# Attention and a two-layer feed-forward block on one core: the seven-product second layer used from the third group of tokens on

## The chip, the core and the metric

One NeuronCore of a Trainium2 chip runs the whole program. TensorE (PE) multiplies matrices, VectorE (DVE) and ScalarE (ACT) work element by element, GpSimd (POOL) does additions in on-chip memory, and SyncE (SP) issues most of the transfers. The metric is device time in microseconds (us); lower is better. About 0.3% (2.5 us) is what a measurement of this kernel can tell from no change.

## The reference, cut to what matters

Attention runs in blocks of 64 tokens in 64 (batch, head) pairs; its output, 4608 tokens of 512 numbers, goes through two weight matrices with a function of one number between them. All in 32-bit floating point.

```python
scores = scale * np.matmul(q_c, k_c.transpose(0, 1, 2, 4, 3))   # blocks of 64 x 64
scores = scores - np.max(scores, axis=-1, keepdims=True)
attn = np.exp(scores)
attn = attn / (np.sum(attn, axis=-1, keepdims=True) + 1e-09)
out = np.matmul(attn, v_c)
...
x = np.ascontiguousarray(attn_out.transpose(0, 2, 1, 3)).reshape(B * S, H * D)   # 4608 x 512
...
h = x @ w_in            # 512 -> 2048: the first layer
g = h - np.tanh(h)
return (g @ w_out).astype(np.float32)   # 2048 -> 512: the second layer
```

## The kernel before, in words

The 4608 tokens are 36 tiles of 128 ("pairs"), in 9 groups of four (`SIZES`). Each group goes through attention, the first layer and the second layer. The 2048 inner columns are 16 blocks of 128 (`FC = 16`); one block of one group is called a unit here. Every 32-bit operand is split into a high part (`h`, `wh`, `gh`, `xh`) and a low rest (`l`, `wl`, `gl`, `xl`), and a product is three matmuls: high by high, high by low, low by high.

There are three ways of doing the two layers.

- Groups 0 and 1: `FeedForward` with both layers in the 32-bit format of TensorE (`F32R`). One unit is `gemm1` (12 matmuls of 512 columns, L572), then `shrink` (tanh on ACT, subtraction on DVE into `t`, L583 and L584), `split` (`gh` on ACT L591, `gl` on DVE L592), and two units later `gemm2` (12 matmuls of 512 columns, L601).
- Group 2: `FeedForward` with `half` set. The first layer takes weights and tokens as pairs of 16-bit numbers, the second layer stays in 32 bits.
- Groups 3 to 8: `Fast`. Both layers take 16-bit pairs, and the second layer is a two-by-two block product done with seven products instead of eight (`Fast.gemm2`, L709: 21 matmuls of 256 columns for two tiles and two blocks of inner columns). GpSimd makes the seven sums of the left operand in every unit (L678 to L680).

What the later ways need is prepared while earlier groups run. `Half.convert` rewrites one block of first-layer weights in 16 bits: two ACT and two DVE instructions (L490, L491, L493, L494); its rest goes over the low part of the same block. `Half.combine` makes the sums of the second-layer weights for a pair of blocks j and j + 8 on GpSimd (L506 to L517), and `Half.shorten` rounds the four sums to 16-bit pairs (ACT L534, DVE L535). Before these, `Half.powers` finds a power of two by which the weights are scaled, from sums of squares (`square`, L110) through a reduction over the partitions on GpSimd. `Late` is the attention of groups 2 to 8: a scale per group (`sums`, `halves`, `across`, `spread_out`), then for each half group b `split` of q, k and v (L353, L354), `scores` on PE (L364), `shifted` (DVE L381, L382), `exponent` (ACT), `totals` (DVE L396), `divided` (DVE L404), `transpose` (ACT, DVE L411 and a transposing transfer) and `values` (PE L364, DVE L432).

In the kernel before, all 16 converts, the attention of group 2 and 16 of the 32 squares lie beside group 1. All combines but the last two and their shortens, and the attention of group 3, lie beside group 2. From group 3 on, only the attention of the next group lies beside the running group.

The order of the instructions has three sources. The first part of the program (up to the bar in `PLAN`) and everything from group 2 on is in written order (`tc.manual_schedule`): every engine takes its instructions in the order in which the code issues them. In between (the rest of group 0 and group 1) a scheduler sets the order by data and rank. In the written part `ahead` and the loops around it put steps into a table `at`: key 2s comes behind `gemm1` and `shrink` of unit s, key 2s + 1 behind the `gemm2` of that unit. `FeedForward.written` is the loop of a unit: split of the unit before, `gemm1`, `shrink`, the steps of 2s, `gemm2` of the unit two back, the steps of 2s + 1. So DVE has, in every unit, first `t`, then what the table put there, then `gl`, then the next `t`.

## Time and profile before

| what | us |
|---|---|
| three runs | 820.85, 820.67, 818.77 (median 820.67) |
| the profiled execution | 818.66, with a span of 816.9 from the first to the last instruction |
| group 0 ends: its first output store | 126.7 from the span's start |
| group 1 ends: its first output store | 219.6 |
| group 2 ends: its last output store | 321.1 |
| last output store issued | 814.0 |
| TensorE busy | 803.5 |
| VectorE busy | 644.5 |
| ScalarE busy | 467.4 |
| GpSimd busy | 381.1 |

The span is what the engines' instructions cover; the remaining 1.8 us of the profiled execution lie around it. TensorE's granted clock is 0.998 of full speed over the span. In the profile's rows "L601 PE MATMUL po<-wh,gh" is line 601, the engine, the operation and output from inputs by tile name. A chain row gives the start, the length and what the end of the program goes back to at that time; a timeline row gives start, length, the instruction, and in brackets the engine's idle time before it and what ended it. A row of the stage table gives the busy time of every engine in a stretch of the span, with the number of instructions in brackets. Two instructions that follow one another at once on one engine overlap by some 0.1 us in the records, so that a sum of lengths is a little above the time taken. One unit (one block of inner columns) is the beat to look for: 16 in each group.

### The profile page before, as it was taken

The page shows a single profiled execution, that of the slowest core. Times are in us where ns is not written, and L with a number is a line of the kernel's source. Part 1 is how long each engine was busy: PE and PEld are TensorE (multiplying, and loading weights), DVE is VectorE, ACT ScalarE, POOL GpSimd, SP SyncE. Part 2 cuts the span into 40 slices and gives each one's busy share as a digit, 9 for nine tenths or more (in the row PEclk, how much of TensorE's full clock was granted, in tenths as well). Part 3 has the DMA queues.
Part 4 walks back from the last instruction along what each step waited for, and adds up shares of the span by engine and source line. Part 5 has one row for each costly group of instructions (what it writes and reads, how often), then busy time and mean ns, then how long its engine had stood idle before and what let it go on. Part 6 is the DMA issues. An engine that isn't in the chain of part 4 may idle for free.

```text
span 816.9 us, 20560 instructions
## 1 busy us (share of the span) xinstructions
PE 803.5 (98%) x8805; PEld 664.6 (81%) x8805; DVE 644.5 (79%) x853; ACT 467.4 (57%) x754; POOL 381.1 (47%) x385
## 2 busy tenths in 40 slices
PE   8999999999999999999999999999999999999997
PEld 5677787788756568888888888888888888888886
DVE  6899986877459999797879787878887887877553
ACT  5698779665345457564745474546554655454332
POOL 2000000000028666856665756575666665757563
PEclk9999999999999999999999999999999999999999
DMA  7954523321201113122222322222222220202000
GB/s 250 344 180 156 187 86 140 105 53 34 71 1 30 49 37 120 27 79 53 80 53 79 53 79 53 79 53 79 52 80 52 79 53 2 53 3 52 2 27 26
DMA packets 58459, 63.19 MB, mean 77 GB/s; under 512 B 32768, under 2 KB 38912, under 8 KB 58368
## 3 DMA queue, kind: packets, MB, share of 16 engines
q1 hardware_dynamic: 57792, 61.10, 25.1%
q8 instruction: 69, 1.13, 0.6%
q10 hardware_dynamic: 576, 0.79, 0.3%
q14 instruction: 22, 0.18, 0.1%
HBM read 45.09 MB, written 9.44 MB: 67 GB/s over the span
## 4 chain that ended last, share of the span: by engine, by line
PE 80%; DVE 10%; ACT 5%; POOL 2%; issue 2%; DVEq 0%; ACTq 0%
PE ph L669 29%; PE po L709 26%; PE po L601 10%; PE ph L572 10%; PE psa L364 3%; PE ph L854 1%; DVE w L151 1%; DVE gl L592 1%; DVE w L152 1%; ACT wh L155 1%; ACT s L228 1%; ACT w L146 1%; ACT junk L110 1%; DVE wh L535 1%; PE psa L193 1%
## 5 line engine op out<-in xcount | busy, mean ns | idle before, releaser
L669 PE MATMUL ph<-xh,wl 128*128 128x256 f16 x2160 | 249.5, 273 | 0.0
L669 PEld LDWEIGHTS <-wl 128*128 128x128 f16 x2160 | 209.8, 98 | 25.2 <-issue 0.5
L678 POOL TENSOR_TENSOR xl<-xl 128x256 f32<-128x256 f32 x96 | 97.1, 1011 | 183.8 <-DVE xl L677 182.9
L676 ACT ACTIVATE t<-ph,sig 128x512 f32<-128x512 f32 x96 | 65.8, 685 | 147.6 <-PE ph L669 146.9
L677 DVE SCALAR_TENSOR_TENSOR xl<-ph,sig,t 128x512 f32<-128x512 f32 x96 | 71.6, 746 | 46.5 <-ACT t L676 46.3
L709 PEld LDWEIGHTS <-wh 128*128 128x128 f16 x1008 | 98.7, 98 | 11.4
L679 POOL TENSOR_TENSOR xl<-xl 128x128 f32<-128x128 f32 x96 | 105.5, 1099 | 0.0
L680 POOL TENSOR_TENSOR xl<-xl 128x256 f32<-128x256 f32 x96 | 93.1, 970 | 0.0
L709 PE MATMUL po<-wl,wh 128*128 128x256 f16 x576 | 89.7, 273 | 0.0
L690 DVE SCALAR_TENSOR_TENSOR wh<-xl,to_g,wh 128x896 f16<-128x896 f32 x48 | 64.6, 1346 | 30.0 <-ACT wh L689 30.0
L689 ACT ACTIVATE wh<-xl,to_g 128x896 f16<-128x896 f32 x48 | 49.9, 1039 | 60.8 <-POOL xl L680 60.8
L601 PE MATMUL po<-wh,gh 128*128 128x512 f32 x192 | 79.5, 414 | 1.0 <-ACT gh L591 0.8
L690 DVE SCALAR_TENSOR_TENSOR gl<-xl,to_g,gh 128x896 f16<-128x896 f32 x48 | 71.8, 1496 | 9.1 <-ACT gh L689 8.9
L601 PE MATMUL po<-wl,gh 128*128 128x512 f32 x192 | 75.7, 394 | 0.9 <-POOL wl L159 0.9
L572 PE MATMUL ph<-xh,wl 128*128 128x512 f16 (+2 forms) x316 | 76.5, 380 | 0.0
L601 PE MATMUL po<-wh,gl 128*128 128x512 f32 x192 | 75.1, 396 | 1.0 <-DVE gl L592 1.0
L709 PE MATMUL po<-wh,wh 128*128 128x256 f16 x432 | 75.9, 273 | 0.0
L709 PEld LDWEIGHTS <-gh 128*128 128x128 f16 x672 | 64.9, 98 | 7.8
L709 PE MATMUL po<-wh,gh 128*128 128x256 f16 x336 | 54.4, 273 | 0.0
L709 PE MATMUL po<-wl,gh 128*128 128x256 f16 x336 | 52.4, 273 | 0.0
L592 DVE TENSOR_TENSOR gl<-t,gh 128x512 fp32r<-128x512 f32 (+1 forms) x50 | 40.0, 800 | 15.5 <-ACT gh L591 15.3
L689 ACT ACTIVATE gh<-xl,to_g 128x896 f16<-128x896 f32 x48 | 49.5, 1032 | 4.2 <-POOL xl L680 4.1
(159 smaller groups left out, 1402.5 us busy)
## 6 DMA issues: line engine op xcount, KB each, us to landing
raw<-w_in SPq DMA_DIRECT2D x16, 512.0 KB, 3.7
raw<-w_out SPq DMA_DIRECT2D x16, 512.0 KB, 4.6
rawk<-kL SPq DMA_DIRECT2D x28, 256.0 KB, 3.9
rawv<-vL SPq DMA_DIRECT2D x28, 256.0 KB, 3.6
xl<-qL SPq DMA_DIRECT2D x28, 256.0 KB, 2.9
out<-wh SPq DMA_DIRECT2D x46, 128.0 KB, 1.8
q<-qE SPq DMA_DIRECT2D x8, 256.0 KB, 5.2
v<-vE SPq DMA_DIRECT2D x8, 256.0 KB, 4.5
```

The source lines that it names most:

```text
L572: nc.tensor.matmul(ph, lhsT=self.weight(fc, 0, a)[:, kc * P:(kc + 1) * P], rhs=x[b][:, kc, cols], start=(k == 0), stop=(k == 3 * KC - 1))
L592: nc.vector.tensor_sub(gl, t, gh)
L601: nc.tensor.matmul(self.po[t], lhsT=gg[a][:, ts], rhs=self.weight(fc, 1, b), start=(fc == 0 and i == 0), stop=(fc == FC - 1 and i == 2))
L669: nc.tensor.matmul(self.ph[:, 1 - f::2, :], lhsT=half_w[fc][:, w, kc * P:(kc + 1) * P], rhs=rhs, start=(k == 0), stop=(k == 3 * KC - 1))
L676: nc.scalar.activation(t, self.ph, AF.Tanh, scale=sig)
L677: nc.vector.scalar_tensor_tensor(out=u[:, :4], in0=self.ph, scalar=sig, in1=t, op0=ALU.mult, op1=ALU.subtract)
L678: nc.gpsimd.tensor_add(u[:, 4:6], u[:, 1:3], u[:, 0:4:3])
L679: nc.gpsimd.tensor_add(u[:, 6], u[:, 1], u[:, 2])
L680: nc.gpsimd.tensor_sub(u[:, 0:4:3], u[:, 0:2], u[:, 2:4])
L689: nc.scalar.activation(gh, u, AF.Copy, scale=powers[1])
L690: nc.vector.scalar_tensor_tensor(out=gl, in0=u, scalar=powers[1], in1=gh, op0=ALU.mult, op1=ALU.subtract)
L709: nc.tensor.matmul(place[m], lhsT=part[:, self.SUM[m]], rhs=w[m][:, o], start=first, stop=(last and part is gl), skip_group_check=True)
```

## The change

`FAST` goes from 3 to 2: group 2 uses `Fast` too, and the way with 16-bit first and 32-bit second layer is gone, with all code that only it used. So everything that `Fast` needs is now prepared beside group 1: all converts, the combines and shortens of the first six pairs of blocks, and the attention of group 2. Group 1 is in written order (`written`), with its blocks taken in the order 0, 8, 1, 9, ... (`ORDER`), so that the two blocks of a pair come free together.

With it come these:

- The attention of group 2 (`late` in `ahead`) starts its half groups at units 4 and 11, not 6 and 14, and its scale is found one to two units sooner.
- The sums of the weights are all taken beside group 0: the squares of the first eight blocks of the second layer on ACT, and for the last eight blocks a maximum of absolute values on DVE. A new step `most` starts the three reductions over partitions on GpSimd one after the other ahead of group 1; `powers` only uses their results. The approximate roots of the sums of squares get a margin of 1 + 2^-8.
- `combine` does its sums in pieces of 256 columns: 9 GpSimd instructions for a pair of blocks instead of 6. Of pair 0 the last step comes one unit later.
- `gemm2` of the 32-bit way takes first all products with `gh`, then those with `gl`.
- The four output copies of group 1 are all on ACT (two were on DVE).
- The loads of group 2's k, v and q are issued in that order, each four at a time. Two more tiles (`SPARE`) give the combines a place.

A convert is put at key 2i - 1, in the unit before the one whose `gemm1` reads the block. Its rest still goes over the low part that this `gemm1` reads, so on DVE the convert of block i + 1, which stands between `t` and `gl` of unit i, waits for `gemm1` of unit i + 1.

```diff
-FAST = 3
+FAST = 2
...
+SQUARED = 8
+ORDER = tuple(i // 2 + i % 2 * FC // 2 for i in range(FC))
...
-        def powers(self, part):
+        def most(self, part):
+
             q, most = sums_w[part], self.pool.tile([P, 1], F32, name=f"most{part}")
...
-            nc.vector.tensor_scalar_mul(q, q, 2.0 ** 64)
+            some = q if part == 0 else q[:, :SQUARED]
...
+            nc.vector.tensor_scalar_mul(some, some, 2.0 ** 64 * (1 + 2.0 ** -8))
             nc.vector.reduce_max(out=most, in_=q, axis=AX.X)
             nc.vector.tensor_scalar_mul(most, most, 2.0 ** -12)
-            power(self.pool, f"w{part}", most, self.to[:, part:part + 1], self.back[:, part:part + 1])
+            top = self.tops[part] = self.pool.tile([P, 1], F32, name=f"top{part}")
+            nc.gpsimd.partition_all_reduce(top, most, channels=P, reduce_op=bass_isa.ReduceOp.max)
+            if part == 0:
+                self.whole = self.pool.tile([P, FC], F32, name="whole")
+                nc.gpsimd.partition_all_reduce(self.whole, q, channels=P, reduce_op=bass_isa.ReduceOp.add)
+
+        def powers(self, part):
+            power_of_two(self.tops[part], self.to[:, part:part + 1], self.back[:, part:part + 1])
...
+            sides = slice(0, HD), slice(HD, DM)
             w1 = place_of(*free[0], F32)
-            nc.gpsimd.tensor_add(w1, h1, l1)
+            for some in sides:
+                nc.gpsimd.tensor_add(w1[:, some], h1[:, some], l1[:, some])
...
-            for t in range(t0, t1):
-                ts = slice((t - t0) * P, (t - t0 + 1) * P)
-                for i, (a, b) in enumerate(((0, 0), (0, 1), (1, 0))):
-                    nc.tensor.matmul(self.po[t], lhsT=gg[a][:, ts], rhs=self.weight(fc, 1, b), start=(fc == 0 and i == 0), stop=(fc == FC - 1 and i == 2))
+            for some in ((0, 0), (0, 1)), ((1, 0),):
+                for t in range(t0, t1):
+                    ts = slice((t - t0) * P, (t - t0 + 1) * P)
+                    for a, b in some:
+                        nc.tensor.matmul(self.po[t], lhsT=gg[a][:, ts], rhs=wt[fc][1][b], start=(fc == 0 and a == b), stop=(fc == FC - 1 and a == 1))
...
-                if t % 2:
+                if t % 2 and self.g == 0:
...
+        late = g == FAST
...
-        put(-3 if g > FAST else 1, 0, att.halves, g, 0)
-        put(2, 1, att.halves, g, 1)
-        put(4, 1, att.across, g)
-        put(5, 1, att.spread_out, g)
+        put(1 if late else -3, 0, att.halves, g, 0)
+        put(2, 0 if late else 1, att.halves, g, 1)
+        put(3 if late else 4, 0 if late else 1, att.across, g)
+        put(3 if late else 5, 1, att.spread_out, g)
...
-        for b, u in enumerate((6, 14)):
+        for b, u in enumerate((4, 11) if late else (6, 14)):
...
     for fc in range(FC):
         square(fc, 0, junk)
+    for fc in range(SQUARED):
+        square(fc, 1, junk)
+    for fc in range(SQUARED, FC):
+        nc.vector.tensor_reduce(out=sums_w[1][:, fc:fc + 1], in_=wt[fc][1][0].bitcast(F32), axis=AX.X, op=ALU.max, apply_absolute_value=True)
...
-    ff = FeedForward(1, x)
-    ff.room(ps_o1, range(2))
-    ff.room(ps_o2, range(2, 4))
-    at[2 * FC].append(lambda: half.powers(1))
-    ff.run([(fc, 0, SIZES[1]) for fc in range(FC)], at)
...
+    at[1] += [lambda: half.powers(0), lambda: half.powers(1)]
+    for i, fc in enumerate(ORDER):
+        at[max(2 * i - 1, 1)].append(lambda i=i, fc=fc: half.convert(fc, place_of("l", 0, ORDER[i - 1]) if i else first_place))
+    at[6].append(for_attention)
...
     for j in range(FC // 2 - 2):
-        at[4 * j + 7].append(lambda j=j: make(j, 5))
+        at[4 * j + 7].append(lambda j=j: make(j, 5 if j else 4))
+        if j == 0:
+            at[9].append(lambda: make(0, 1))
...
     with tc.manual_schedule():
-        ff = FeedForward(FAST - 1, nx)
+        for part in range(2):
+            half.most(part)
+        ff = FeedForward(1, nx)
         ff.room(ps_o1, range(2))
         ff.room(ps_o2, range(2, 4))
-        for s in range(FC):
-            ff.written(s, s // 2 + s % 2 * FC // 2, at)
+        for s, fc in enumerate(ORDER):
+            ff.written(s, fc, at)
+        ff.split()
```

How it moves instructions is seen at three places. The first is VectorE in one middle unit of the last group in the 32-bit way, from `t` to the next `t`, the unit in which attention's scaling (`divided`) stands. Before, in group 2 (line 581 is `t`, 404 the scaling, 535 the shortens, 592 `gl`; the numbers behind an underscore only tell tiles apart):

```order
L581 SCALAR_TENSOR_TENSOR t<-ph,sig,t 128x512
L404 TENSOR_TENSOR s<-s,sm 128x1024
L535 SCALAR_TENSOR_TENSOR wl_3043<-wh_3036,to_w,wl_3043 128x512
L535 SCALAR_TENSOR_TENSOR wh_3044<-wh_3033,to_w,wh_3044 128x256
L592 TENSOR_TENSOR gl<-t,gh 128x512
```

Now, in group 1 (line 522 is `t`, 365 the scaling, 484 the shortens, 438 and 439 a convert, 530 `gl`):

```order
L522 TENSOR_TENSOR t<-ph,t 128x512
L365 TENSOR_TENSOR s<-s,sm 128x1024
L484 SCALAR_TENSOR_TENSOR wl_1890<-wh_1882,to_w,wl_1890 128x512
L438 SCALAR_TENSOR_TENSOR wl_2138<-wh_1097,to_w,wl_2135 128x512
L439 TENSOR_TENSOR wl_2135<-wl_2135,wl_2138 128x512
L484 SCALAR_TENSOR_TENSOR wh_1821<-wh_1878,to_w,wh_1821 128x256
L530 TENSOR_TENSOR gl<-t,gh 128x512
```

The two instructions of a convert stand between `t` and `gl`; there is one convert in every unit up to the fifteenth.

The second place is TensorE in one `gemm2` of the 32-bit way. Before (line 601; `po` are the four output tiles, `wh` and `wl` the weights), the last three output tiles of a unit:

```order
L601 MATMUL po_2726<-wh_1082,gh 128x512
L601 MATMUL po_2726<-wl_1083,gh 128x512
L601 MATMUL po_2726<-wh_1082,gl 128x512
L601 MATMUL po_2727<-wh_1082,gh 128x512
L601 MATMUL po_2727<-wl_1083,gh 128x512
L601 MATMUL po_2727<-wh_1082,gl 128x512
L601 MATMUL po_2728<-wh_1082,gh 128x512
L601 MATMUL po_2728<-wl_1083,gh 128x512
L601 MATMUL po_2728<-wh_1082,gl 128x512
```

Now (line 540), a whole unit:

```order
L540 MATMUL po_1597<-wh_1099,gh 128x512
L540 MATMUL po_1597<-wl_1100,gh 128x512
L540 MATMUL po_1598<-wh_1099,gh 128x512
L540 MATMUL po_1598<-wl_1100,gh 128x512
L540 MATMUL po_1599<-wh_1099,gh 128x512
L540 MATMUL po_1599<-wl_1100,gh 128x512
L540 MATMUL po_1600<-wh_1099,gh 128x512
L540 MATMUL po_1600<-wl_1100,gh 128x512
L540 MATMUL po_1597<-wh_1099,gl 128x512
L540 MATMUL po_1598<-wh_1099,gl 128x512
L540 MATMUL po_1599<-wh_1099,gl 128x512
L540 MATMUL po_1600<-wh_1099,gl 128x512
```

The first matmul that reads `gl` was the third of the twelve and is now the ninth.

The third place is VectorE at the end of group 0, around the last conversion of raw weights. Before (line 152 ends the joining of the raw words, 159 makes a low part, 584 `t`, 592 `gl`, 467 to 470 begin `powers`):

```order
L152 SCALAR_TENSOR_TENSOR w<-raw,w 128x1024
L592 TENSOR_TENSOR gl<-t,gh 128x512
L159 TENSOR_TENSOR wl_1109<-w,wh_1108 128x512
L159 TENSOR_TENSOR wl_1111<-w,wh_1110 128x512
L584 TENSOR_TENSOR t<-ph,t 128x512
L467 TENSOR_SCALAR sums_102<-sums_102 128x16
```

Now (137, 144, 522, 530 and 407 are the same steps, 841 is the new maximum):

```order
L137 SCALAR_TENSOR_TENSOR w<-raw,w 128x1024
L841 TENSOR_REDUCE sums_103<-wh_1087 128x1
L522 TENSOR_TENSOR t<-ph,t 128x512
L144 TENSOR_TENSOR wl_1110<-w,wh_1109 128x512
L144 TENSOR_TENSOR wl_1112<-w,wh_1111 128x512
L530 TENSOR_TENSOR gl<-t,gh 128x512
L841 TENSOR_REDUCE sums_103<-wh_1091 128x1
L841 TENSOR_REDUCE sums_103<-wh_1095 128x1
L841 TENSOR_REDUCE sums_103<-wh_1099 128x1
L841 TENSOR_REDUCE sums_103<-wh_1103 128x1
L841 TENSOR_REDUCE sums_103<-wh_1107 128x1
L522 TENSOR_TENSOR t<-ph,t 128x512
```

Six of the eight maxima stand behind the last conversion of raw weights (one more follows the rows shown), one just ahead of it and one further up.

More of the change, by code (lines that the diff above doesn't have):

```diff
@@ L81, in attn_ffn_kernel @@
     wt, half_w, fast_w, w_pool = [[None, None] for _ in range(FC)], [None] * FC, {}, {}
+    SPARE = range(FC, FC + 2)
     def weight_tiles(pool, fcs):
@@ L553, in __init__ @@
             self.g, self.x, self.queue, self.po, self.ready = g, x, [], [], None
-            self.half = g > 1
-            if g > 1:
-                self.sig = half.power_of(g)[0]
-        def weight(self, fc, part, i):
-            return half_w[fc][:, i] if self.half and part == 0 else wt[fc][part][i]
         def room(self, pool, tiles):
@@ L623, in written @@
                 self.split()
-            if unit is not None:
-                self.gemm1(unit, 0, SIZES[self.g])
-                self.shrink()
+            self.gemm1(unit, 0, SIZES[self.g])
+            self.shrink()
             for f in at.pop(2 * s, []):
                 f()
-            if len(self.queue) > (unit is not None):
+            if len(self.queue) > 1:
                 self.gemm2()
```

160 lines of the change are left out of this document (38 added, 122 removed).

## The prediction

> **What bounds the kernel now.** The page comes first: busy time by engine, then the chain of waits.
>
> ```profile
> span 816.9 us, 20560 instructions
> PE 803.5 (98%) x8805; PEld 664.6 (81%) x8805; DVE 644.5 (79%) x853; ACT 467.4 (57%) x754; POOL 381.1 (47%) x385
> PE 80%; DVE 10%; ACT 5%; POOL 2%; issue 2%; DVEq 0%; ACTq 0%
> ```
>
> PE is the bound overall, but 10% of the chain lies on DVE. The view by stretches tells where. The rows are group 1; group 2 from its unit 5 on, where the combines run; the first units of group 3; and a whole later group.
>
> ```profile
> 128.00:221.00 93.00, 93.00 (x770) 74.77 (x769) 66.56 (x114) 59.43 (x96) 1.94 (x2) 1.00 0.21 62
> 245.80:305.20 59.40, 58.37 (x443) 36.64 (x441) 56.30 (x65) 31.68 (x49) 43.69 (x32) 1.00 0.13 37
> 305.20:354.00 48.80, 46.84 (x658) 40.56 (x658) 43.10 (x53) 31.97 (x44) 35.05 (x34) 1.00 0.29 80
> 500.00:583.00 83.00, 82.95 (x1104) 73.53 (x1102) 68.21 (x82) 44.54 (x56) 52.48 (x55) 1.00 0.23 64
> ```
>
> The columns behind the length are PE, weight loads, DVE, ACT, POOL. PE is dense in groups 1 and 4 to 8. In the second row DVE is busy 56.30 of 59.40 us: it is all but the second bound there. What a block of matmuls costs is read from the chain in order of time (start, length, what):
>
> ```profile
> 150.42 2.80 PE ph L572 x12
> 153.23 2.80 PE po L601 x12
> 203.49 2.72 PE ph L572 x12
> 282.88 2.60 PE ph L572 x12
> 285.49 2.79 PE po L601 x12
> 299.06 0.91 PE psa L364 x96
> 354.19 2.62 PE ph L669 x24
> 356.81 2.29 PE po L709 x21
> ```
>
> The first three are group 1 (32 bits), the next two group 2, the last two a unit of the seven-product way. PE's own timeline shows two waits from group 1 on that are longer than 0.3 us:
>
> ```profile
> 280.32 0.50 PE L601 MATMUL po<-wh,gl 128*128 128x512 f32 x1 [1.03 <-DVE gl L592]
> 350.86 0.94 PE L364 MATMUL psa<-a,wh 64*64 64x64 f16 x92 [1.94 <-DVE a L354]
> ```
>
> Both wait for DVE, and both lie where combines run.
>
> **The change part by part.**
>
> *PE, group 2.* A unit was 2.60 + 2.79 = 5.39 us and becomes 2.62 + 2.29 = 4.91. Sixteen units give back 16 x 0.48 = **-7.7 us**. Attention's matmuls (0.91 a set) are as many as before. All 12-matmul blocks of group 1 may now take 2.80, as the first ones did, while the 14 or so later ones took 2.72 in a stretch without shortens and combines: 14 x 0.08 = **+1.1**, with 0 at the other end. Group 2's own 32-bit block at 2.79 speaks for the 1.1.
>
> *DVE, group 1 from unit 5 to 15.* The comparison is with the same units of group 2 in the kernel before, where DVE was busy 56.30 us with the same combines and shortens beside it. Added are ten converts and the maxima, shift, sum and scaling of attention's second half group, which the earlier unit 11 pulls in; one `split` goes out to unit 4.
>
> ```profile
> L493 DVE SCALAR_TENSOR_TENSOR wl<-wh,to_w,wl x15: 741/746/753, 135.2 to 210.8; 128x512 f16<-128x512 f32 x15
> L494 DVE TENSOR_TENSOR wl<-wl,wl x15: 410/424/428, 136.0 to 211.6; 128x512 f16<-128x512 f16 x15
> 149.06 1.28 DVE L354 SCALAR_TENSOR_TENSOR a<-rawk,to,a 128x1024 f16<-128x1024 f32 x1
> L381 DVE TENSOR_REDUCE mx<-psa 128x16 f32<-128x1024 f32 x1 | 1.2, 1212 | 0.0
> L382 DVE TENSOR_TENSOR s<-psa,mx 128x1024 f32<-128x1024 f32 x1 | 1.2, 1224 | 0.0
> L396 DVE TENSOR_REDUCE sm<-s 128x16 f32<-128x1024 f32 x1 | 1.2, 1209 | 0.0
> L404 DVE TENSOR_TENSOR s<-s,sm 128x1024 f32<-128x1024 f32 x1 | 1.2, 1208 | 0.0
> ```
>
> A convert is 0.75 + 0.42, of which about 0.09 overlaps with a neighbour: 1.08, ten make 10.8. The four attention steps are 4.9, the small ones behind the sum 0.3. One `split` less is -1.2. So DVE needs 56.3 + 10.8 + 5.2 - 1.2 = 71.1 us. PE needs eleven units of 5.60 and three sets of 0.91: 64.3. DVE falls **6.8 us behind**.
>
> How much of this PE feels is the slack between them. `t` of a unit can start 2.80 us after the unit's `gemm1` began plus a tanh of 0.60 (row below): 3.4. The `gl` just ahead of it in DVE's order is wanted in the next unit, behind `gemm1` (2.80) and now also behind the eight products with `gh` (8 of 12 of 2.80 = 1.87): 5.60 + 4.67 = 10.3. So DVE may be 6.9 us late for nothing; with the old order of products it would have been 5.5. But it starts late: the convert in unit 4 waits for `gemm1` of unit 5, and behind it stand the convert (1.08), a `split` (1.2) and `gl` (0.6), where only a tanh would have passed: 2.9 - 0.6 = 2.3. So 6.8 + 2.3 - 6.9 = **+2.2 us** of stall in group 1. The stall of 1.03 in group 2 is gone with its cause: **-1.0**.
>
> ```profile
> L583 ACT ACTIVATE t<-ph 128x512 f32<-128x512 f32 x30 | 18.0, 599 | 15.8 <-PE ph L572 15.8
> L107 ACT ACTIVATE t<-rawk 128x2048 uint8<-128x2048 f32 x6 | 11.4, 1900 | 0.0
> L490 ACT ACTIVATE wl<-wh,to_w 128x512 f16<-128x512 f32 x15 | 10.8, 717 | 1.5 <-DVE wl L494 1.2
> ```
>
> This takes DVE's waits for POOL as they were. Their size is the unknown. In the same stretch (groups of DVE and POOL, 245.8 to 305.2) and in the timelines of both:
>
> ```profile
> L592 DVE TENSOR_TENSOR gl<-t,gh 128x512 fp32r<-128x512 f32 x10 | 12.8, 1280 | 0.0
> 309.63 0.68 DVE L592 TENSOR_TENSOR gl<-t,gh 128x512 fp32r<-128x512 f32 x1
> 252.84 1.27 DVE L535 SCALAR_TENSOR_TENSOR wh<-wh,to_w,wh 128x512 f16<-128x512 f32 x1
> 254.03 1.74 DVE L354 SCALAR_TENSOR_TENSOR wh<-xl,to,wh 128x1024 f16<-128x1024 f32 x1
> 255.70 1.50 DVE L535 SCALAR_TENSOR_TENSOR wh<-wh,to_w,wh 128x256 f16<-128x256 f32 x1
> 257.13 1.78 DVE L592 TENSOR_TENSOR gl<-t,gh 128x512 fp32r<-128x512 f32 x1
> 252.82 0.75 POOL L515 TENSOR_TENSOR wh<-wh 128x256 f32<-128x256 f32 x1
> 253.51 1.18 POOL L517 TENSOR_TENSOR wh<-wh,wh 128x256 f32<-128x256 f32 x1
> 254.66 2.26 POOL L506 TENSOR_TENSOR wh<-wh,wl 128x512 f32<-128x512 f32 x1
> ```
>
> `gl` alone is 0.68; here it is 1.28 on average and 1.78 behind a POOL addition of 512 columns. The `split` behind one of 256 columns takes 1.74, not 1.28: 0.46 more. The two engines take turns. From below: smaller pieces could halve the waits, and then no stall is left, 0. From above: each of the twenty new DVE instructions waits for one piece of 256 columns, 20 x 0.46 = 9.2 us more, all beyond the slack: 2.2 + 9.2 = 11.4. I take the waits as they were, since POOL's additions are as many columns as before and only the turns are shorter.
>
> The Trainium skill (SBUF - State Buffer, section "Who interferes with whom") says of this that a VectorE instruction with two SBUF inputs and a GpSimd instruction that reads SBUF exclude each other for a whole instruction. By that rule the upper end, 11.4, is the one to expect. The trace agrees for single instructions (1.78 against 0.68), but with a mean of 1.28 only about half of the turns collide.
>
> *ACT and POOL.* Ten converts bring ACT 10 x 1.43 = 14.3 us (two instructions of 0.717, the second taken like the first) to the 31.68 of the second stretch: 46 of 64, covered by PE. Uncovered it would cost nothing until 64 is passed. Cutting POOL's additions costs a fixed part each; POOL is busy 43.69 of 59.40 and stays inside. The group's copies on ACT and the load order cost nothing: they lie beside 8 us of `gemm1` in front of the first `gemm2`. The last q load stands on SP's queue behind three stores that wait for group 0's copies, and its first reader is in unit 1; uncovered it would delay attention's scale, the next term.
>
> *Start of group 1.* The scale of group 2's attention is wanted on PE right behind `gemm1` of unit 3, in front of a `gemm2`. ACT's two sums of 1.90 are in units 1 and 2 behind converts. What queues behind the transpose is `gemm2` of unit 1. Between 0 and one such sum, 1.9; I take **+0.9**.
>
> *End of group 0.* Eight maxima of 512 columns are new on DVE; the nearest row is the maximum over 1024 columns, 1.2 us, so some 0.6 each.
>
> ```profile
> 293.80 1.20 DVE L312 TENSOR_REDUCE v<-rawv 128x1 f32<-128x1024 f32 x1
> 122.92 0.69 DVE L584 TENSOR_TENSOR t<-ph,t 128x512 f32<-128x512 f32 x1 [2.44 <-ACT t L583]
> 124.80 0.69 DVE L592 TENSOR_TENSOR gl<-t,gh 128x512 fp32r<-128x512 f32 x1 [1.18 <-ACT gh L591]
> ```
>
> Six stand where DVE idles 2.44 and 1.18 us, the other two in the full stretch before: at most 1.2, and PE had work there. I take **+0.5**, between 0 and 8 x 0.6 = 4.8. The eight later squares on ACT only go; the reductions on POOL run beside the first `gemm1`.
>
> *Start of the seven-product way.* In units 16 to 22 DVE has 6.3 us less than before (maxima, shift, sum, scaling and two copies have moved), but enters up to 6.9 late instead of about 1.6. I leave the stall of 1.94 as it is: **0**, between -1.9 and +2.
>
> The sum: -7.7 + 1.1 + 2.2 - 1.0 + 0.9 + 0.5 = **-4.0**. Against the profiled execution of 818.66 that is 814.7. That execution is at the low end of the runs (818.77 to 820.85), so I put the time at **815.5 us**.
>
> **The rivals.**
>
> *DVE and POOL block each other and bound group 1.* The upper end above: stall 11.4 instead of 2.2, -4.0 + 9.2 = +5.2, so 824 to 826. For it: DVE at 95% in the second row, two stalls there. Against it: with all this PE lost only 1.03 us in group 2. It decides from 6.5 us more waiting on (-4.0 + 6.5 = +2.5). The page of the Trainium skill named above states this case as its rule.
>
> *The moved maxima hold up the end of group 0.* All 4.8 us on the path, and the start of group 1 at its 1.9: -4.0 + 4.3 + 1.0 = +1.3, so about 820: no change. For it: the third place in the listing, where a maximum stands ahead of the last conversion. Against it: DVE's idle time in the rows above.
>
> *The waits shrink with the pieces.* No stall in group 1, none at 350.86, all matmul blocks as fast as before: -4.0 - 2.2 - 1.9 - 1.1 = -9.2, so 809.5. For it: a turn of 256 columns delays an instruction by 0.46, one of 512 by 1.78 - 0.68 = 1.10. Against it: there are more turns.
>
> **How the numbers follow.** The forecast (811 to 818.5) has a chance of 0.48, the first rival 0.20, the second 0.17, the third 0.15. No change is 818.2 to 823.1 against the median of 820.67, the 0.3% that a measurement can tell. Faster: nearly all of the forecast (0.43) and the third rival, 0.58. Slower: the first rival, with the little by which the second can go beyond, less what of the first stays inside, 0.20. Same: the rest, 0.22. The range of 808.5 to 823 holds the forecast and the third rival, most of the second and a little of the first. The forecast's own range is 811 to 818.5.
>
> **What would show it.** Right: in the profile after, seven groups with units of 4.91; in group 1 units of 5.60, DVE over 95% busy from unit 5 on, and PE waits for `gl` of 1 to 4 us in units 12 to 15, little before. Wrong: units of group 1 longer than 6 us one after the other, with PE waiting for DVE in each (first rival); the last `gemm2` of group 0 later than in the profile before by 2 us or more (second); no wait of PE for `gl` at all (third). PE waits over 2 us on anything else would upset all of it.

## The result: 826.28 us, 0.9% slower

The changed kernel takes 826.28 us (median of four runs, 826.03 to 828.52) against 819.72 for the kernel before in the same series (818.72 to 820.85). The ratio is 1.0086, with a 95% interval of 1.0061 to 1.0111. The forecast was 815.5 us, and faster. All ratios below are to the kernel before, run beside each version.

The page of the kernel after, its first lines and its chain of waits by engine:

```profile
span 824.5 us, 21334 instructions
PE 800.5 (97%) x9141; PEld 684.4 (83%) x9141; DVE 665.2 (81%) x868; ACT 470.8 (57%) x744; POOL 436.0 (53%) x463
PE 79%; DVE 11%; ACT 5%; POOL 3%; issue 2%; DMA 1%; SPq 0%; DVEq 0%; ACTq 0%
```

PE is busy 3.0 us less than before, and the span is 7.6 longer: PE idles 24.0 us (span less busy time), not 13.4. The stretches (length; busy time of PE, weight loads, DVE, ACT, POOL; granted clock behind them) show where:

```profile
126.50:154.80 28.30, 24.13 (x98) 18.74 (x97) 18.01 (x39) 17.65 (x28) 7.47 (x10) 0.94 0.14 47
154.80:231.40 76.60, 68.38 (x555) 54.01 (x554) 71.23 (x87) 45.85 (x74) 48.15 (x49) 0.96 0.19 49
300.00:383.00 83.00, 82.95 (x1104) 73.52 (x1103) 68.39 (x83) 45.05 (x56) 53.20 (x55) 1.00 0.24 65
```

The first two rows are group 1: units 0 to 4, then 5 to 15. A later group takes 83.0 us as before. So nearly all of it lies in group 1. In PE's timeline from there on these are the waits over 0.3 us:

```profile
135.88 0.50 PE L540 MATMUL po<-wh,gh 128*128 128x512 f32 x1 [1.32 <-ACT gh L529]
144.55 0.37 PE L296 MATMUL psa<-ident,sums 128*3 128x128 f32 x1 [2.85 <-ACT t L521]
183.92 1.20 PE L540 MATMUL po<-wh,gl 128*128 128x512 f32 x4 [1.11 <-DVE gl L530]
190.85 1.19 PE L540 MATMUL po<-wh,gl 128*128 128x512 f32 x4 [1.07 <-DVE gl L530]
198.56 2.01 PE L540 MATMUL po<-wh,gl 128*128 128x512 f32 x4 [1.97 <-DVE gl L530]
214.82 0.97 PE L333 MATMUL psa<-a,wh 64*64 64x64 f16 x96 [4.08 <-DVE xh L390]
275.15 0.94 PE L333 MATMUL psa<-a,wh 64*64 64x64 f16 x92 [1.42 <-DVE a L323]
```

Six waits in group 1 make 12.4 us. The largest is in front of the scores of the second half group: they stand one `gemm1` behind the values of the first, both use the one tile `psa`, and the copy that frees it (L390) is late on DVE. PE ends the values at 207.8, and the second half of the copy ends at 214.7:

```profile
206.82 0.98 PE L333 MATMUL psa<-s,wh 64*64 64x64 f16 x96
213.98 0.69 DVE L390 SCALAR_TENSOR_TENSOR xh<-psa,xh 128x512 f16<-128x512 f32 x1 [0.66 <-ACT xh L389]
```

Something else makes PE slower there. The rows below are PE alone (length, busy, granted clock), cut at the points where the clock changes:

```profile
195.30:198.70 3.40, 1.44 (x7) 0.99 0.43 79
198.70:202.10 3.40, 3.40 (x9) 0.50 0.00 0
208.90:212.30 3.40, 1.84 (x9) 1.00 0.20 68
212.30:215.70 3.40, 0.88 (x96) 1.00 0.31 77
215.70:219.10 3.40, 3.40 (x19) 0.50 0.19 19
219.10:222.50 3.40, 3.40 (x16) 0.99 0.82 274
```

Behind three of the waits the clock is halved for 3.4 us (the third such stretch begins at 144.1). At half clock PE does about half the work (9 matmuls in 3.4 us instead of 16): 1.7 us are lost in each of the two stretches shown, 1.5 in the third, where PE still idles for 0.45, so 4.9 in all.

### The profile page after: what moved, and what is told of

Read it like the earlier page. It is cut to its first block, busy times and chain, and to the rows that moved or that the text cites. A ratio compares the mean times of both kernels' runs of the same rounds, so it can differ in the third digit from the quotient of the medians.

```text
span 824.5 us, 21334 instructions
## 1 busy us (share of the span) xinstructions
PE 800.5 (97%) x9141; PEld 684.4 (83%) x9141; DVE 665.2 (81%) x868; ACT 470.8 (57%) x744; POOL 436.0 (53%) x463
## 4 chain that ended last, share of the span: by engine, by line
PE 79%; DVE 11%; ACT 5%; POOL 3%; issue 2%; DMA 1%; SPq 0%; DVEq 0%; ACTq 0%
PE ph L590 33%; PE po L630 30%; PE po L540 6%; PE ph L514 5%; PE psa L333 3%; DVE gl L530 1%; DVE wl L438 1%; DVE wh L484 1%; DVE wl L484 1%; PE psa L178 1%; POOL xl L599 1%; ACT junk L108 1%; DMA q<-qE 1%; DVE t L522 1%; DVE wl L439 1%
## 5 line engine op out<-in xcount | busy, mean ns | idle before, releaser
L590 PE MATMUL ph<-xh,wl 128*128 128x256 f16 x2520 | 291.3, 273 | 0.0
L590 PEld LDWEIGHTS <-wl 128*128 128x128 f16 x2520 | 244.9, 98 | 29.3 <-issue 0.5
L599 POOL TENSOR_TENSOR xl<-xl 128x256 f32<-128x256 f32 x112 | 109.5, 978 | 215.0 <-DVE xl L598 214.9
L630 PEld LDWEIGHTS <-wh 128*128 128x128 f16 x1176 | 115.0, 98 | 13.3
L600 POOL TENSOR_TENSOR xl<-xl 128x128 f32<-128x128 f32 x112 | 124.0, 1107 | 0.0
L601 POOL TENSOR_TENSOR xl<-xl 128x256 f32<-128x256 f32 x112 | 107.4, 959 | 0.0
L630 PE MATMUL po<-wl,wh 128*128 128x256 f16 x672 | 104.6, 273 | 0.0
L540 PE MATMUL po<-wh,gh 128*128 128x512 f32 x128 | 53.8, 420 | 2.1 <-ACT gh L529 1.9
L540 PE MATMUL po<-wl,gh 128*128 128x512 f32 x128 | 52.2, 408 | 0.9 <-POOL wl L144 0.9
L630 PEld LDWEIGHTS <-gl 128*128 128x128 f16 x392 | 38.4, 98 | 4.4
L540 PE MATMUL po<-wh,gl 128*128 128x512 f32 x128 | 36.8, 405 | 4.1 <-DVE gl L530 4.1
```

The source lines that it names most:

```text
L540: nc.tensor.matmul(self.po[t], lhsT=gg[a][:, ts], rhs=wt[fc][1][b], start=(fc == 0 and a == b), stop=(fc == FC - 1 and a == 1))
L590: nc.tensor.matmul(self.ph[:, 1 - f::2, :], lhsT=half_w[fc][:, w, kc * P:(kc + 1) * P], rhs=rhs, start=(k == 0), stop=(k == 3 * KC - 1))
L599: nc.gpsimd.tensor_add(u[:, 4:6], u[:, 1:3], u[:, 0:4:3])
L600: nc.gpsimd.tensor_add(u[:, 6], u[:, 1], u[:, 2])
L601: nc.gpsimd.tensor_sub(u[:, 0:4:3], u[:, 0:2], u[:, 2:4])
L630: nc.tensor.matmul(place[m], lhsT=part[:, self.SUM[m]], rhs=w[m][:, o], start=first, stop=(last and part is gl), skip_group_check=True)
```

## The experiments

There are two lines of theory. **Place**: each stop of PE comes from a step that stands too near to another in the written order, and can be moved. **Capacity**: DVE has more to do in group 1 than there is time for, and a stop that is moved comes back elsewhere.

### What GpSimd's reads cost (e4)

This version leaves out the sums of the first six pairs: GpSimd fills their places with a constant. The edit is the same for all nine instructions of `combine`; the first is shown.

```diff
+            def made(f, out, *ins):
+                if j < 6:
+                    nc.gpsimd.memset(out, 0.01)
+                else:
+                    f(out, *ins)
...
-                nc.gpsimd.tensor_add(w1[:, some], h1[:, some], l1[:, some])
+                made(nc.gpsimd.tensor_add, w1[:, some], h1[:, some], l1[:, some])
```

> The sums of the first six pairs of blocks are left out: GpSimd fills their places with a constant, in as many instructions and the same places, so it writes but does not read. The outputs of groups 2 to 8 are not those of the reference. Theory A (DVE's two-input instructions are held by GpSimd's reads): gl falls from 1.2 to about 0.7 us, the three waits for gl and the wait of 4.08 in front of the scores go, with the two slow stretches behind them: 826.3 - 4.2 - 1.7 - 5.8 = 814.6; the wait of 2.85 at the start of the group stays. Theory B (order and chains alone, no exclusion): gl stays at 1.2, 825 to 826.

Measured: 812.61 us, ratio 0.9911 (0.9895 to 0.9927), 13.7 below the changed kernel and 2 below theory A. Units 5 to 15 of this version, with as many instructions on PE, DVE and ACT, and its waits of PE from unit 5 to group 3:

```profile
152.50:217.70 65.20, 64.44 (x555) 51.90 (x555) 56.36 (x87) 46.28 (x74) 14.53 (x48) 1.00 0.23 58
202.72 0.97 PE L333 MATMUL psa<-a,wh 64*64 64x64 f16 x96 [0.76 <-DVE xh L390]
261.42 0.94 PE L333 MATMUL psa<-a,wh 64*64 64x64 f16 x92 [1.35 <-DVE a L323]
```

65.2 us instead of 76.6, and DVE needs 56.4 for what took it 71.2. Which instructions shrink is read from DVE's timeline, first of the kernel after, then of this one:

```profile
179.20 0.85 DVE L439 TENSOR_TENSOR wl<-wl,wl 128x512 f16<-128x512 f16 x1
179.97 1.21 DVE L357 TENSOR_REDUCE sm<-s 128x16 f32<-128x1024 f32 x1
182.66 1.21 DVE L530 TENSOR_TENSOR gl<-t,gh 128x512 fp32r<-128x512 f32 x1
183.79 0.68 DVE L522 TENSOR_TENSOR t<-ph,t 128x512 f32<-128x512 f32 x1
```

```profile
174.29 0.42 DVE L439 TENSOR_TENSOR wl<-wl,wl 128x512 f16<-128x512 f16 x1
174.63 1.22 DVE L357 TENSOR_REDUCE sm<-s 128x16 f32<-128x1024 f32 x1
177.12 0.68 DVE L537 TENSOR_TENSOR gl<-t,gh 128x512 fp32r<-128x512 f32 x1
177.72 0.68 DVE L529 TENSOR_TENSOR t<-ph,t 128x512 f32<-128x512 f32 x1
```

Instructions with two inputs in on-chip memory (L439, `gl`) take nearly double beside GpSimd's sums. The reduction, with one input, and `t`, whose `ph` lies in PSUM, take the same. The Trainium skill (SBUF - State Buffer, "Who interferes with whom") says that these two kinds part in this way; the runs agree, 1.21 against 0.68 and 0.68 against 0.68. The fills are also shorter than the sums (POOL 14.5 us instead of 48.2); this run doesn't part the two.

### Longer turns (e3)

Three of the five sums go over 512 columns at once; the other two keep their 256.

```diff
-            sides = slice(0, HD), slice(HD, DM)
+            sides = (slice(0, DM),)
...
```

> Three of the sums of a pair are again taken over 512 columns at once, six GpSimd instructions instead of nine. Theory A: the columns are as many and DVE and POOL exclude each other for as long as before; within 1.5 us of 826.3, gl in group 1 at 1.2 to 1.3 us in the mean. Theory B (turns cost): each of the 18 turns fewer in group 1 gives DVE back up to 0.46 us, 8.3 in all; the waits for gl (4.2) and the slow stretch behind the third (1.7) go, 818 to 821.

Measured: 829.95 us, 1.0123 (1.0107 to 1.0140): 3.7 slower, outside both. The cut into pieces of 256 is the part of the change that helps: beside 512 columns the stop at the scores is 6.56 us, and single instructions wait longer (the longest L439 takes 1.40 instead of 0.85). Not all do: the mean of `gl` in group 1 (150 to 240) is 0.82 us here and 0.97 in the kernel after.

### One place moved at a time (e2, e1, e9)

```diff
-        put(3 if late else 4, 0 if late else 1, att.across, g)
-        put(3 if late else 5, 1, att.spread_out, g)
+        put(4, 0 if late else 1, att.across, g)
+        put(4 if late else 5, 1, att.spread_out, g)
```

> The transpose of the sums (across) and the one behind it (spread_out) stand in unit 4 instead of 3. Theory A (place): the wait of 2.85 us at 144.55 goes, and the half clock behind it (1.7): 826.3 - 4.5 = 821.8; the split of the first half group, in the same unit, is later by less than DVE's idle time there. Theory B (capacity): what is not done on DVE in units 3 and 4 is missing later; the waits for gl (1.11, 1.07, 1.97) grow by up to 2.7 and 824 to 826 stays.

```diff
-        for b, u in enumerate((4, 11) if late else (6, 14)):
+        for b, u in enumerate((4, 12) if late else (6, 14)):
```

> The second half group of group 2's attention starts at unit 12 instead of 11; nothing else is moved. Theory A (place): PE's wait of 4.08 us in front of the scores comes from the fixed order alone. The scores stand one gemm1 behind the values of the first half group, and both use the one tile psa, whose copy into xl stands far back in DVE's order. With three keys between them instead of one the wait goes, and with it the stretch of half clock behind it (3.4 us at 0.50, worth 1.7): 826.3 - 5.8 = 820.5. Theory B (capacity): DVE has more to do than there is time for, so the lateness shows at the next place where PE waits for it: a wait for gl in units 13 to 15 or for a in the first units of group 2 grows by about as much, 825 to 827.

```diff
-            at[o + 2 * u + 17].insert(0, lambda b=b: att.values(g, b, xs[g]))
+            at[o + 2 * u + (15 if late and b == 0 else 17)].insert(0, lambda b=b: att.values(g, b, xs[g]))
```

> The values of the first half group of group 2 stand one unit earlier (key 23 instead of 25), so that on DVE their copy into xl stands ahead of the splits of the second half group and no longer between them. No work is left out. Theory A (place): the scores of the second half group find psa free, the wait of 4.08 us and its slow stretch (1.7) go, 820.5. Theory B (capacity): DVE stays as late as before, the waits for gl behind it or for a in the scores grow, as when the half group was moved: 825 to 828.

Measured: e2 824.22 us, 1.0057 (1.0037 to 1.0077); e1 831.60, 1.0140 (1.0121 to 1.0159); e9 826.72, 1.0085 (1.0070 to 1.0100). PE's waits at the scores in e2, at the scores and in group 2 in e1, and at the scores in e9:

```profile
212.58 1.50 PE L333 MATMUL psa<-a,wh 64*64 64x64 f16 x96 [6.00 <-DVE xh L390]
```

```profile
219.61 1.44 PE L333 MATMUL psa<-a,wh 64*64 64x64 f16 x92 [2.95 <-DVE a L323]
248.24 2.78 PE L590 MATMUL ph<-xh,wl 128*128 128x256 f16 x24 [1.79 <-DVE xl L598]
260.73 0.37 PE L296 MATMUL psa<-ident,sums 128*3 128x128 f32 x1 [4.22 <-DVE xh L390]
```

```profile
214.54 1.44 PE L333 MATMUL psa<-a,wh 64*64 64x64 f16 x92 [3.08 <-DVE a L323]
```

e2 and e9 lie in the range of theory B (capacity), e1 4.6 us above it. With the later scale, the stop of 2.85 and its half clock go (unit 5 begins at 150.42 instead of 154.84), and the stop at the scores grows from 4.08 to 6.00: 2.1 are kept. With the values earlier the scores no longer wait for the copy but for the split behind it. With the half group later a stop at the scores stays, its work meets the first units of group 2 besides, and the run is 5.3 longer than the kernel after.

### DVE's own idle time (e5, e6)

DVE's waits in group 1 of the kernel after (what waits for what, total, times, longest):

```profile
DVE wl L438 <- PE ph L514: 8.4, 3, 4.5
DVE wl L438 <- ACT wl L436: 2.6, 3, 1.5
```

An engine with too much to do stands idle for 8.4 us, behind its own order: the convert of a block waits for a `gemm1` that PE reaches late. Most of it lies at the start: 4.46 in front of the convert at 151.38 and 2.65 in front of the one at 156.97, where PE is late from the stop of 2.85 (which ended with ACT's tanh) and its half clock. The third, 1.29 at 222.28, lies behind the stop at the scores, where PE had waited for DVE.

```diff
-        at[max(2 * i - 1, 1)].append(lambda i=i, fc=fc: half.convert(fc, place_of("l", 0, ORDER[i - 1]) if i else first_place))
+        at[max(2 * i, 1)].append(lambda i=i, fc=fc: half.convert(fc, place_of("l", 0, ORDER[i - 1]) if i else first_place))
```

e6 is this edit and that of e2.

> Every convert is put one key later: block i behind gemm1 and shrink of unit i (key 2i) and no longer in the unit before. On DVE its first instruction (L438), which writes over the low part that gemm1 of block i reads, then stands behind t of unit i, which needs the same gemm1, and has nothing of its own to wait for. Theory A (DVE is short of time and stands idle in its own order): the 8.4 us that DVE idles in front of L438 come back to it; the waits of PE for gl (4.2 us), the wait in front of the scores (4.1) and the two slow stretches behind them (3.4) shrink or go: 815 to 820. Theory B (DVE idles there only because PE is late by itself; what holds PE is the exclusion by GpSimd): the waits for gl and in front of the scores stay within 1.5 us of what they were, 825 to 828.

> The converts one key later as in the run before it, and across and spread_out in unit 4 as in the run with the scale a unit later. Theory A: the wait of 2.85 us and its slow stretch (1.7) go too and nothing comes back elsewhere, since DVE has room again: 4.5 us below the run with the converts alone, 811 to 816. Theory B (capacity in group 1 is what counts, the places where PE stops are its outlets): only the 2 us that the later scale gave alone, 823 to 826.

Measured: e5 824.55 us, 1.0054 (1.0036 to 1.0071); e6 820.85, 1.0012 (1.0003 to 1.0022). In e5 the wait for `gemm1` is gone from DVE's list, the waits for `gl` fall from 4.2 to 2.1, but the one at the scores grows to 7.87, with half clock for another 4.8 us behind it: 1.7 us are won, a time near theory B's, while the waits moved as neither said. With the later scale (e6) 3.7 more are won, nearer to the 4.5 of theory A; the time lies between the two ranges. The two together give 5.4, more than 2.1 and 1.7.

### The order of the products (e7)

```diff
-            for some in ((0, 0), (0, 1)), ((1, 0),):
-                for t in range(t0, t1):
+            for t in range(t0, t1):
+                for some in ((0, 0), (0, 1)), ((1, 0),):
```

> The products of a gemm2 in the order of the kernel before: tile by tile, high by high, high by low, low by high, so gl is wanted 6 matmuls (1.4 us) sooner. Theory A (DVE is behind and PE meets it at gl): the lateness is felt 1.4 us sooner, the first wait for gl comes earlier than 183.9 and the total grows by 1.4 to 4: 827.7 to 830. Theory B (the stops are at fixed places and do not depend on the slack): within 1 us of 826.3.

Measured: 824.40 us, 1.0060 (1.0041 to 1.0078), a miss for both: 1.9 faster. The waits for `gl` from unit 5 on are two of 1.89 and 1.29 instead of 1.11, 1.07 and 1.97. The gain is at the start: waits of 0.88 and 1.13 in the first `gemm2` take the place of 1.32 and 2.85. So the 1.4 us of slack that I gave the new order cannot be seen in the time. Why the start is shorter can be read from the clock. The transpose of the scale, at which the kernel after waits 2.85, starts at about the same time in both (144.17 here, 144.55 there). Here the half clock lies ahead of it, from 138.4 to 141.8, where PE would have waited anyway; in the kernel after it lies behind it, from 144.1 on.

### The halved clock (e8)

```diff
+    zeros = late.tile([P, P], F32R, name="zeros", bufs=1)
+    nc.vector.memset(zeros.bitcast(F32), 0.0)
+
+    def fill(n):
+        for i in range(n):
+            nc.tensor.matmul(ff.po[i % 4], lhsT=zeros, rhs=wt[ORDER[15]][1][0], start=False, stop=False)
...
+    at[26].append(lambda: fill(14))
```

> Fourteen matmuls of 512 columns with a left operand of zeros, added to the group's own sums, stand in front of the scores of the second half group: they run while PE would wait there. Theory A (the granted clock is halved for 3.4 us behind a stretch in which PE idled over about half of the time): PE then idles at most 1 us there, the clock stays at 1.00 from 212 to 220, and the run is 1.7 us shorter: 824.6, though PE does 3.2 us more work. Theory B (the clock falls for another reason, the scores' form or DVE's load): it is at 0.50 behind the scores all the same, 826 to 828.

Measured: 825.71 us, 1.0072 (1.0051 to 1.0092). PE's timeline at that place, and PE's clock in two stretches:

```profile
209.49 3.43 PE L857 MATMUL po<-wh,zeros 128*128 128x512 f32 x14
215.61 0.97 PE L333 MATMUL psa<-a,wh 64*64 64x64 f16 x96 [2.69 <-DVE xh L390]
```

```profile
199.00:202.00 3.00, 2.98 (x13) 1.00 0.00 0
216.00:218.00 2.00, 2.00 (x77) 1.00 0.03 8
```

Behind the scores the clock stays full, as theory A says, although PE still idled 2.69 us and not the 1 us expected. Also behind the wait at 199.02 it stays full here. But two stretches of half clock less give only 0.6 us, not 3.4, and not the 1.7 of theory A: the scores start 0.8 later than in the kernel after (0.5 of it is there before, at the wait for `gl`), although the clock was full all the way from there, since PE waits for DVE. Half clock costs where PE is the bound, and little where it would wait next anyway.

### The places together (e10, e11, e12, e17)

e10 has the edits of e5, e2 and e9 (converts, scale, values). e11 is e10 with the sums in pieces of 128 columns, e12 is e10 with the edit of e1, e17 is e10 with the scores of the second half group, and what follows them, a unit later and its values at key 41:

```diff
-            sides = slice(0, HD), slice(HD, DM)
+            sides = [slice(i, i + P) for i in range(0, DM, P)]
...
```

```diff
-            put(u + 2, 0, att.scores, g, b)
+            u2 = u + (late and b)
+            put(u2 + 2, 0, att.scores, g, b)
...
-            at[o + 2 * u + (15 if late and b == 0 else 17)].insert(0, lambda b=b: att.values(g, b, xs[g]))
+            at[o + 2 * u + ((19 if b else 15) if late else 17)].insert(0, lambda b=b: att.values(g, b, xs[g]))
```

> Converts a key later, scale a unit later, values of the first half group a unit earlier, together. With the first two alone the only stop over 2 us left was that in front of the scores (7.87 us, with 5 us lost by the half clock behind it). Theory A (place, now that DVE has its idle time back): most of it goes, 820.85 - 7.9 - up to 5.1: 808 to 813. Theory B (capacity): half or more of it comes back at gl or a, 815 to 820.

> The run before it with the sums in pieces of 128 columns. With 512 instead of 256 the changed kernel was 3.7 us slower. Theory A (each turn of GpSimd delays a waiting DVE instruction by its own length, so shorter turns delay less): a further 1 to 3 us less than the run before it. Theory B (the columns decide; more instructions bring GpSimd their fixed part): 0 to 2 us more than the run before it.

> The three places, and the second half group from unit 12 on. Theory A (DVE has room again in group 1): within 1.5 us of the three places alone. Theory B (what is moved out of group 1 meets the last two combines and the first units of group 2, where DVE is full too): 3 to 6 us more, as the move alone gave 5.3 over the changed kernel.

> The same places (scores a unit later, values of the second half group a unit later), with the converts left in group 1, behind gemm1 of their unit. Theory A (place decides): like e16 within 2 us. Theory B (DVE's total in group 1 decides): the waits for gl (2.1 us) stay or grow and the scores still stop PE: 3 to 7 us above e16, 815 to 820.

Measured: e10 819.22 us, 0.9998 (0.9989 to 1.0008); e11 819.69, 1.0003 (0.9992 to 1.0013); e12 824.91, 1.0067 (1.0052 to 1.0082); e17 825.06, 1.0069 (1.0048 to 1.0090). Units 5 to 15 of e10, and its waits there over 2 us:

```profile
149.30:225.40 76.10, 67.34 (x556) 53.64 (x556) 72.39 (x95) 49.06 (x77) 47.17 (x49) 0.96 0.18 49
205.31 0.22 PE L333 MATMUL psa<-a,wh 64*64 64x64 f16 x4 [3.75 <-ACT a L322]
208.44 1.44 PE L333 MATMUL psa<-a,wh 64*64 64x64 f16 x92 [2.91 <-DVE a L323]
```

The 7.1 us against the kernel after are won at the start of group 1 (unit 5 begins at 149.3 instead of 154.8) and in group 2, where the wait of 1.42 at 275.15 is gone. Units 5 to 15 take 76.1 instead of 76.6, with two places in them moved: here DVE is the bound, as theory B has it. Pieces of 128 end the waits for `gl` (its mean 0.90 us, 1.04 in e10), but POOL is then busy 24.84 of 25 us and the attention of group 3 stops PE; the time is the same. e12 is 5.7 above e10 and has two stops in the first units of group 2, of 1.67 and 4.23.

### Work taken out of the full stretch (e13, e14, e15, e16, e18)

e13 is e10 with this, and with other tiles for the seven-product way to take over:

```diff
+    LATER = {8: 27, 9: 29, 10: 30, 11: 31, 12: 34, 13: 35, 14: 40, 15: 42}
...
-        at[max(2 * i, 1)].append(lambda i=i, fc=fc: half.convert(fc, place_of("l", 0, ORDER[i - 1]) if i else first_place))
+        at[LATER.get(i, max(2 * i, 1))].append(lambda i=i, fc=fc: half.convert(fc, place_of("l", 0, ORDER[i - 1]) if i else first_place))
```

e14 is e13 with the later scores of e17, e15 is e13 with pieces of 128, e16 is e14 with the values of the second half group at key 41. e18 is e13 with this (the splits of k and v move with that of q):

```diff
-    LATER = {8: 27, 9: 29, 10: 30, 11: 31, 12: 34, 13: 35, 14: 40, 15: 42}
+    LATER = {8: 26, 9: 27, 10: 28, 11: 29, 12: 30, 13: 31, 14: 40, 15: 42}
...
-            put(u, 1, att.split, g, b, "q")
+            early = u - (late and b)
+            put(early, 1, att.split, g, b, "q")
...
-                if t % 2 and self.g == 0:
+                if t % 2:
```

> The three places, and the converts of the last eight blocks later: those of blocks 8 to 11 of the order at the end of group 1 (keys 27 to 31), the last four in the first units of group 2 (keys 34, 35, 40, 42); the tiles that the seven-product way takes over are others accordingly. A convert costs DVE 1.5 us beside the sums (0.90 + 0.62). Theory A (DVE's total in units 5 to 13 is the cause): six converts less there, 9 us, end the waits for gl (2.1) and most of that in front of the scores (6.7, with 3.5 of half clock): 819.2 - 8 to 12, 807 to 811; DVE idled 6.7 us between 225 and 250, so the four that land there cost at most 2. Theory B (the place decides, or the first units of group 2 are as full): 816 to 821.

> As the run before it, with the scores of the second half group and what follows them a unit later, its splits left where they are. Theory A (DVE has room now): within 1.5 us of the run before it, or 2 to 4 less if PE still stopped there. Theory B (the first units of group 2 are full): 2 to 5 more, as the later half group was in both earlier runs.

> The converts out of the way as in e13, with the sums in pieces of 128 columns. Theory A (shorter turns help where DVE is full, GpSimd had 22.08 of 25 us in the stretch behind group 1 with them): 1 us less to 2 us more than e13. Theory B (columns and the fixed part of more instructions decide): 3 us or more above e13, with PE waiting for GpSimd's sums or for a in the first units of group 2.

> As the run with the converts out of the way and the scores a unit later, with the values of the second half group one unit later too (key 41 instead of 39): in that run PE's one long stop was 6.39 us in front of these values, for the transposing transfer, with 3.4 us lost by two slow stretches. Theory A (place, DVE has room): most of it goes, 821.2 - 6 to 9 = 812 to 815, the first version below the kernel before. Theory B (capacity): it comes back in front of the attention of group 3 or at xl, 818 to 822.

> As the run with the converts out of the way (e13, 820.3), with these differences: two of the four output copies of group 1 on DVE again, only the last two converts in group 2 (the six before them in units 13 to 15 of group 1), and the splits of the second half group one unit earlier, scores and values where they were. Theory A (ACT's queue sets the start of group 2, and scores stop PE only for late splits): the stop of 2.49 us at xl in the first units of group 2 shrinks by 1 to 2, the stop of 3.08 at the scores goes with its slow stretch (1.7): 814 to 817. Theory B (DVE is full from unit 5 on, so splits a unit earlier come out no earlier): the stop at the scores stays over 2 us or waits for gl of 1 to 2 us come back in units 9 to 11: 818 to 822.

Measured: e13 820.32 us, 1.0005 (0.9994 to 1.0016); e14 821.17, 1.0022 (1.0013 to 1.0032); e15 821.56, 1.0015 (1.0004 to 1.0026); e16 824.80, 1.0061 (1.0041 to 1.0082); e18 819.27, 1.0003 (0.9994 to 1.0013). Waits of e13, of e16 and of e18:

```profile
202.81 0.94 PE L333 MATMUL psa<-a,wh 64*64 64x64 f16 x92 [3.08 <-DVE a L323]
238.85 1.36 PE L594 MATMUL ph<-xh,wl 128*128 128x256 f16 x11 [2.49 <-DVE xl L602]
```

```profile
241.19 5.03 PE L594 MATMUL ph<-xh,wl 128*128 128x256 f16 x24 [7.33 <-DVE xl L602]
255.67 0.27 PE L296 MATMUL psa<-ident,sums 128*3 128x128 f32 x1 [3.96 <-DVE xh L390]
```

```profile
236.87 2.78 PE L594 MATMUL ph<-xh,wl 128*128 128x256 f16 x24 [1.54 <-DVE xl L602]
266.51 1.44 PE L333 MATMUL psa<-a,wh 64*64 64x64 f16 x92 [1.59 <-DVE a L323]
```

In e13 no wait for `gl` is left, so converts out of the way do what theory A says there. The first units of group 2 take the gain back. e14 and e15 stay within 1.3 us of e13. e17 (converts in their place) and e16 are equal, so there the converts are not what decides; e16 is above both of its ranges. In e18 PE does not stop at the scores of group 1 any more and the stop at `xl` is 1.54, as theory A says; two waits for `gl` of 1.1 stay.

Where the gain goes is seen from the first `gemm1` of group 2, in e10, e13 and e18:

```profile
225.24 1.48 PE L590 MATMUL ph<-xh,first_place 128*128 128x256 f16 x12
219.19 1.48 PE L594 MATMUL ph<-xh,first_place 128*128 128x256 f16 x12
215.38 1.49 PE L594 MATMUL ph<-xh,first_place 128*128 128x256 f16 x12
```

Unit 5 begins at 149.4 to 149.7 in all three, so units 5 to 15 take 75.9, 69.6 and 65.7 us. e18 is there as short as the run without the sums (65.0). The rest of the program takes 591.7, 599.6 and 603.2: what is taken out of group 1 comes back behind it, and the spans are 816.9, 818.8 and 818.6.

In e16 both long stops lie in the first units of group 2. ACT's timeline there, from e14, which differs only in the place of the values:

```profile
233.71 1.90 ACT L105 ACTIVATE t<-xl 128x2048 uint8<-128x2048 f32 x1
235.62 2.02 ACT L562 COPY wh<-po 128x512 f32<-128x512 f32 x4
237.51 0.74 ACT L435 ACTIVATE wl<-wh,to_w 128x512 f16<-128x512 f32 x1
238.75 0.69 ACT L601 ACTIVATE t<-ph,sig 128x512 f32<-128x512 f32 x1
```

A sum for group 3, four output copies and a convert stand in front of the tanh that starts the unit. So that stretch was no free room: DVE had idle time there, and ACT, after 5.2 us of waiting for GpSimd's sums, works from 230.6 to 242.8 without a gap.

No version that does all the work is faster than the kernel before by more than can be measured. e10, e11, e13 and e18 are the same as it.

## Why the prediction was wrong

Term by term, in us, the measured ones from the profiled executions of both kernels:

| term | predicted | measured | from |
|---|---|---|---|
| PE, group 2 | -7.7 | about -7.7 | later groups at 83.0; not measured apart |
| blocks of 2.80 | +1.1 | about +0.6 | 2.80, 2.76, 2.73 in turn in the chain of the fill run |
| waits of PE, units 5 to 15 | +2.2 | +8.2 | 1.11, 1.07, 1.97, 4.08 |
| the wait of 1.03 before | -1.0 | -1.0 | |
| start of group 1 | +0.9 | +4.2 | 1.32 and 2.85 |
| end of group 0 | +0.5 | -1.2 | first `gemm1` of group 1 at 126.54, before 127.72 |
| start of the seven-product way | 0 | -0.5 | 1.42 instead of 1.94 |
| half clock | none | +4.9 | three stretches of 3.4 at 0.50, 0.45 of the first idle |
| sum | -4.0 | +7.5 | the spans differ by +7.6 |

- **The step that failed is "So DVE may be 6.9 us late for nothing", in the sum 6.8 + 2.3 - 6.9 = +2.2.** DVE's need in units 5 to 15 came out at 71.23 for 71.1 (by luck, see below), against 64.3 of PE (64.44 in the fill run). Two things were wrong with taking 6.9 off once at the end. First, the need is not spread evenly: `t` of unit 5 starts 1.7 us later than it could (159.90 against 154.84 + 3.4), `t` of unit 8 already 7.9 (183.79 against 172.49 + 3.4), since the three units between take DVE 8.0 each and not 71.1 / 11 = 6.5. At `gl` the slack holds (7.9 - 6.9 = 1.0, and PE waits 1.11), but it is used up in unit 9 and not in units 12 to 15; the three waits for `gl` make 4.15. Second, it holds at `gl` alone: at the scores, PE waits for a copy that stands behind other DVE work, one `gemm1` (2.8 us) away, and stops there for 4.08. Together 8.2 instead of 2.2.
- **Slack that is used up is a debt.** Where e16, e17 and e18 took the stop at the scores away, it was paid in the first units of group 2 (stops of 7.33 and 3.96, 4.36 and 2.89; in e18 11.5 us more than in e10 from there on), which I had put at 0. Without the 6.9 the sum is -4.0 + 6.9 = +2.9.
- **A term was missing: half clock behind a wait, +4.9.** With both, the sum is +7.8. That this is near +7.6 is in part luck, since the other errors cancel: +3.3, -0.5, -1.7 and -0.5 in the table, and 8.2 in place of 9.1. The 4.9 is what the busy time holds; the run with zeros shows that taking two of the stretches away gives 0.6.
- **The start of group 1** was put at 0.9 within 0 to 1.9 and took 4.2. I had priced one sum of 1.90 on ACT; ACT also had converts and the tanh and `gh` of the units in front of the transpose.
- **"I take the waits as they were"** came out by two errors that cancel. A convert in units 4 to 15 takes 0.91 + 0.67, overlap taken off 1.5 and not 1.08; `gl` has a mean of 0.97 and not 1.28, for which the shorter turns are no explanation: with 512 columns (e3) it is 0.82.
- **First rival** (DVE and POOL block each other; 824 to 826): its time and its bound are right. In the fill run DVE needs 14.9 us less in these units; that run doesn't part GpSimd's reads from the shorter fills. The sign I gave for it, every unit over 6 us, is wrong: PE ran dense in between and stopped at four places. I had given it 0.20 because PE lost only 1.03 us in group 2 of the kernel before; there 56.30 us of DVE's work in 59.40 still fitted. **Second rival** (the maxima hold up group 0): wrong, that end is 1.2 us earlier; why stays open. **Third rival** (waits shrink with the pieces): right in sign for the time from 512 to 256 columns, 3.7 us, and too small to decide; from 256 to 128 the time stays the same, and the mean of `gl` doesn't follow the pieces (0.82 with 512 and 0.97 with 256 columns; in e10 and e11 1.04 with 256 and 0.90 with 128).

## What to carry to other kernels

Slack between two engines is to be counted at every place where the one waits for the other, with the smallest taken, and what is used of it is only lent: the next stage has to have room to pay it back. When work is packed beside a stage, add up the engine that comes second with its instructions as long as they are beside its neighbours; at 71 us of work for 64 us of time the whole difference and more is lost, and moving steps out of that stretch only moves the stop. An engine that is short of time and still waits in its own order is worth mending, but the wait is not its worth: the 8.4 us here gave 1.7 alone, and 3.7 more once PE's stop ahead of it was gone too.

## What the runs showed of the hardware

The clock falls behind waits much shorter than I would have guessed, and not behind every one. The stretches of half clock begin at 144.1, 198.7 and 215.7 and last 3.4 us; 54.6 and 17.0 between them are 16 and 5 times 3.41. In windows of that length, the ones in which PE idled over half (58% before 198.7, 74% before 215.7) are followed by a window at half clock, the one with 46% (208.9 to 212.3) is not. One wait of 1.97 us inside a window was enough, and 2.69 us in the run with zeros, split between two windows, were not. In the other runs the border also lies near one half, but it is not sharp: 50% idle was followed by half clock in e7 (135.0 to 138.4) and not in e8 (197.3 to 200.7), 55% not in e11 (197.7 to 201.1), and in e18 a window that was at half clock already was followed by another with only 24% idle (265.7 to 269.1). What the clock goes by beside PE's idle time stays open. The Trainium skill (TensorE: Matmul & The Clock Gate, "Part 1: The HAM clock gate") has the free-running window of this length and half clock after an idle window; the traces agree on the length, and show that the window need not be idle as a whole.
